# Second gate's logits from scaled, split 16-bit rows, in 16-bit transposes and products, tiles staggered in beats

## The chip, the cores and the metric

One core of one Trainium2 chip. The metric is the device time of one execution in microseconds, median of several runs. The core has five engines, each with an instruction queue that runs in order: TensorE (PE; PEld is its weight load), VectorE (DVE), ScalarE (ACT), GpSimd (POOL) and SyncE (SP, which here issues transfers).

## What is computed

Local attention, then a dense mixture of experts with gates from a Sinkhorn iteration, then a second mixture that routes each row to one expert under a capacity. N = 2304 rows of D = 512, E = 8 experts, hidden size F = 1024.

```python
def _moe2_ref(x, w_gate, w1, w2):
    logits = x @ w_gate
    order = np.argsort(-logits.flatten())
    ...
    for idx in order:
        tok, e = (int(idx) // E, int(idx) % E)
        if assigned[tok] >= 0 or counts[e] >= cap:
            continue
        assigned[tok] = e
        counts[e] += 1
    ...
    for e in range(E):
        mask = assigned == e
        h = np.maximum(x[mask] @ w1[e], 0.0)
        out[mask] = h @ w2[e]
```

x of this function is the output of the dense mixture, `out += P[:, e:e+1] * (relu(x @ w1[e]) @ w2[e])` over the eight experts. The change touches `logits = x @ w_gate` and the form in which x is written out for the routed rows.

## The kernel before, in words

The 2304 rows stand as 18 tiles of 128 rows (NT = 18), three tiles to a block (TB = 3). The dense mixture runs expert by expert. `layer1s` (L845) is a first layer in 192-column products of 16-bit high and low halves (`prod`, L865), whose partial sums ScalarE evacuates as `sa`, `sb`, `sc` and writes out as the 16-bit `hh`, while VectorE writes the low half `hl` (L746, L747). `layer2` (L943) makes 24 products of 128x512 for one tile, and VectorE adds the scaled result to the 32-bit accumulator `acc` (L959). After the last expert, number 7, a tile of `acc` is final and is noted in `finals`.

The gate of the second mixture is made beside expert 7, from three places:

- `held_gate` (L1012) goes over the last six tiles (HELD, tiles 12 to 17) before expert 7 has been added to them, and puts partial logits into `lgh`. `held_weights` and `held_logits` later add expert 7's share, so that the logits of these tiles are there before the tiles are.
- `finish_all` (L973) goes over tiles 0 to 11 as they become final: `gate2` for the logits, then `to_rows`.
- `rest` (L1557) does `to_rows` for the six held tiles, at the end of expert 7, beside the start of the routing.

`gate2` (L981) does four 32-bit transposes of a tile on TensorE (L986), a ScalarE evacuation into the scratch `tmp[:, 0]` (L987), eight product instructions in 32 bits with the gate's weights (L991) and a VectorE copy of the eight logits (L992). `to_rows` (L994) prepares the row for the routed layer: ScalarE's sum of squares (L998, whose elementwise result goes to the scratch `tmp[:, 1]`), five small VectorE instructions that make a power-of-two scale of it (`norm_pow2`, L312 to L317), a 16-bit scaled copy into a row buffer `st2k` (L1005), a 32-bit scaled copy into `tmp[:, 1]` (L1006), GpSimd's subtraction of the two, which is the low half of the row (L1008), and a transfer to `xrows` in HBM (L1009). There are four buffers `st2k` (L334).

The order of all this is set in program order. The background generators are advanced by ticks: `layer2` ticks after each three products, `stream` 2.3 ticks for each third slot of `layer1s`, and `yield n` in a generator lets n ticks go by. So a yield is a number of the main work's instructions, not a time. From `man.close()` (L1552) on a scheduler orders the instructions: that covers `held_logits`, the routing and `rest`.

## Time and profile before

| | us |
|---|---|
| median of 3 runs | 1948.85 |
| lowest, highest | 1943.12, 1950.79 |
| profiled execution, device time | 1943.79 |
| its span, first to last instruction | 1942.0 |
| TensorE busy | 1859.8 (96%) |
| VectorE busy | 1261.4 (65%) |
| ScalarE busy | 916.1 (47%) |
| GpSimd busy | 110.8 (6%) |
| mean granted TensorE clock | 0.988 |

The span is that of the profiled execution; its device time is 1.79 us longer. Busy shares are means over stages with different limits: the dense mixture's last expert lies around 1420 to 1636 us, the routing and the hand-over to the routed layers at about 1630 to 1660 us, the routed layers behind that. What is worth a microsecond has to be read from the stage in which it lies. A busy time of TensorE from products counts their modelled ends, which overlap; where the text needs what a product costs it takes the distance between starts.

### The profile page before, as it was taken

How to read it: one execution, taken by the hardware profiler on the slowest of the kernel's cores; microseconds unless marked ns; L12 is line 12 of the kernel's file. 1: busy time of each engine (PE TensorE's matmuls, PEld its weight loads, DVE VectorE, ACT ScalarE, POOL GpSimd, SP SyncE). 2: the span in 40 equal slices, each digit the busy share in tenths (PEclk: the TensorE clock that was granted, in tenths of full speed). 3: DMA queues.
4: the chain of work that ended last, by engine and by line, in shares of the span. 5: the costliest groups of instructions: out<-in, count | busy, mean ns of one | idle time of the engine just before them, and what ended most of it. 6: DMA issues, size and time to landing. Idle time of an engine off the chain costs nothing.

```text
span 1942.0 us, 39658 instructions
## 1 busy us (share of the span) xinstructions
PE 1859.8 (96%) x15605; PEld 1339.3 (69%) x15605; DVE 1261.4 (65%) x3845; ACT 916.1 (47%) x2493; POOL 110.8 (6%) x142
## 2 busy tenths in 40 slices
PE   6899999999999999999999999999999997899987
PEld 5777755776686766767766867677686773676765
DVE  7877796464666676676667666766747777465540
ACT  6777634552455555554554555455534442222222
POOL 0000000000000000000000000000000113223231
PEclk9999999999999999999999999999999998899999
DMA  8465301140134323323442434234231101435451
GB/s 188 89 131 120 83 1 44 59 160 1 55 120 143 119 93 118 138 88 116 145 136 83 131 117 145 93 99 157 88 104 28 43 20 64 175 123 172 159 211 29
DMA packets 172795, 203.32 MB, mean 105 GB/s; under 512 B 83000, under 2 KB 130104, under 8 KB 168512
## 3 DMA queue, kind: packets, MB, share of 16 engines
q1 hardware_dynamic: 164928, 157.78, 27.4%
q0 software_dynamic: 7680, 43.02, 6.3%
q8 instruction: 122, 2.00, 0.4%
q14 instruction: 65, 0.53, 0.1%
HBM read 143.05 MB, written 57.71 MB: 103 GB/s over the span
## 4 chain that ended last, share of the span: by engine, by line
PE 71%; DVE 11%; issue 6%; DMA 5%; ACT 4%; POOL 2%; SPq 0%; POOLq 0%; ACTq 0%; DVEq 0%
PE p L943 28%; PE p L865 17%; PE pb L865 12%; PE p L1302 4%; PE p L773 3%; DMA w2scr<-st2k 2%; DVE st2k L347 1%; DMA raw<-xrows,idx 1%; PE pb L1152 1%; DVE xl L645 1%; PE p L1314 1%; DMA raw<-in_moe_w_dram 1%; DMA ws<-st2k 1%; PE pb L632 1%; DVE pn L605 1%
## 5 line engine op out<-in xcount | busy, mean ns | idle before, releaser
L943 PE MATMUL p<-w2b,hh 128*128 128x512 f16 x2304 | 686.0, 379 | 0.0
L943 PE MATMUL p<-w2b,hl 128*128 128x512 f16 x1152 | 436.6, 379 | 0.0
L943 PEld LDWEIGHTS <-hh 128*128 128x128 f16 x2304 | 222.1, 99 | 218.2 <-issue 0.2
L865 PEld LDWEIGHTS <-w1b 128*128 128x128 f16 x4032 | 340.3, 98 | 22.2 <-issue 4.0
L865 PEld LDWEIGHTS <-w1x 128*128 128x128 f16 x3024 | 256.3, 98 | 21.1 <-issue 7.4
L865 PE MATMUL p<-th,w1x 128*128 128x192 f16 x1344 | 221.2, 246 | 4.3 <-ACT sa L877 2.2
L865 PE MATMUL pb<-xh,w1b 128*128 128x192 f16 x1344 | 221.3, 246 | 0.0
L943 PEld LDWEIGHTS <-hl 128*128 128x128 f16 x1152 | 112.6, 98 | 135.5 <-issue 0.6
L865 PE MATMUL pb<-xl,w1b 128*128 128x192 f16 x672 | 165.3, 246 | 0.0
L865 PE MATMUL p<-tl,w1x 128*128 128x192 f16 x672 | 165.3, 246 | 0.0
L347 DVE SCALAR_TENSOR_TENSOR st2k<-raw,wsc,st2k 128x512 f16<-128x512 f32 x128 | 91.9, 748 | 51.8 <-ACT st2k L345 51.5
L345 ACT ACTIVATE st2k<-raw,wsc 128x512 f16<-128x512 f32 x128 | 86.5, 713 | 71.3 <-DMA ws<-st2k 58.8
L959 DVE SCALAR_TENSOR_TENSOR acc<-p,SE,acc 128x512 f32<-128x512 f32 x126 | 94.0, 746 | 38.2 <-PE p L943 37.8
L1008 POOL TENSOR_TENSOR st2k<-tmp,st2k 128x512 f16<-128x512 f32 x18 | 24.7, 1370 | 1592.2 <-ACT tmp L1006 1571.1
L746 ACT ACTIVATE hh<-sb 128x192 f16<-128x192 f32 x168 | 61.0, 363 | 111.8 <-DVE sb L909 111.8
L865 PE MATMUL p<-th,w1b 128*128 128x192 f16 x672 | 110.6, 246 | 2.9 <-ACT sc L898 2.9
L746 ACT ACTIVATE hh<-sa 128x192 f16<-128x192 f32 x168 | 60.9, 363 | 107.2 <-DVE sa L883 107.2
L865 PE MATMUL pb<-xh,w1x 128*128 128x192 f16 x672 | 110.6, 246 | 0.0
L865 PE MATMUL p<-xh,w1b 128*128 128x192 f16 x672 | 110.6, 246 | 0.0
L883 DVE TENSOR_TENSOR sa<-pb,sa 128x192 f32<-128x192 f32 x168 | 60.0, 357 | 75.1 <-PE pb L865 72.6
L747 DVE SCALAR_TENSOR_TENSOR hl<-sa,hh 128x192 f16<-128x192 f32 x168 | 60.3, 359 | 72.1 <-ACT hh L746 72.1
L747 DVE SCALAR_TENSOR_TENSOR hl<-sb,hh 128x192 f16<-128x192 f32 x168 | 60.3, 359 | 71.7 <-ACT hh L746 71.7
(309 smaller groups left out, 3381.3 us busy)
## 6 DMA issues: line engine op xcount, KB each, us to landing
raw<-in_moe_w_dram SPq DMA_DIRECT2D x128, 512.0 KB, 5.6
ws<-st2k SPq DMA_DIRECT2D x128, 256.0 KB, 4.5
w2b<-w2scr SPq DMA_DIRECT2D x28, 512.0 KB, 7.1
w2scr<-st2k SPq DMA_DIRECT2D x48, 256.0 KB, 4.5
xrows<-st2k SPq DMA_DIRECT2D x18, 257.0 KB, 3.3
vs<-in_v_dram SPq DMA_DIRECT2D x35, 128.0 KB, 4.1
ldq<-in_q_dram SPq DMA_DIRECT2D x16, 256.0 KB, 4.6
ldk<-in_k_dram SPq DMA_DIRECT2D x16, 256.0 KB, 4.8
```

What stands on the lines that cost most here:

```text
L345: A.activation(hi, src, AF.Copy, scale=sc)
L347: V.scalar_tensor_tensor(lo, src, sc, hi, op0=OP.mult, op1=OP.subtract)
L605: V.tensor_tensor_reduce(pn[:, b, hp], pss[:, hp], mk, 1.0, -3.0e38, OP.add, OP.max, mx[:, u:u + 1])
L746: A.activation(hh[:, f, cols], src, AF.Relu)
L747: V.scalar_tensor_tensor(hl[:, f, cols], src, 0.0, hh[:, f, cols], op0=OP.max, op1=OP.subtract)
L773: PE.matmul(p[:, 0:w], w1v[wi][:, c, fs], x[:, c, ts], start=(n == 0), stop=(n == 3 * DC - 1))
L865: PE.matmul(bank[:, 0:HB], aq[wi][:, c, fs], xq[xi][:, c], start=(start and n == 0), stop=(n == 5), skip_group_check=True)
L883: V.tensor_tensor(t, b3[:, 0:HB], t, OP.add)
L943: PE.matmul(p, h[:, f, js], w2v[wi][:, f], start=(n == 0), stop=(n == 3 * FC - 1))
L959: V.scalar_tensor_tensor(acc[:, i], p, SE[:, e, i:i + 1], acc[:, i], op0=OP.mult, op1=OP.add)
L1008: G.tensor_tensor(xr[:, DM:2 * DM], xs, xr[:, 0:DM], OP.subtract)
L1302: PE.matmul(p[:, 0:CAP], wv1[f // 4][w][:, c, fs], xt[:, x * DC + c], start=(n == 0), stop=(n == 3 * DC - 1))
```

## The change

`gate2` becomes one pass for logits and rows. A tile goes through four steps, each issued one beat (BEAT = 3 ticks) after the one before it: (1) ScalarE's sum of squares; (2) the scale on VectorE, the 32-bit scaled copy, the 16-bit scaled copy, GpSimd's subtraction, and for tiles 0 to 11 the transfer to `xrows`; (3) eight 16-bit transposes of high and low half on TensorE and one ScalarE evacuation of 1024 16-bit values; (4) eight 16-bit products with the gate's weights, which are split in two 16-bit halves once by `gate2_weights` (with a reduction over partitions on GpSimd), and two VectorE instructions that undo the scales. Tiles overlap: with each beat all tiles that are under way take their next step, and a new tile is started. The order inside a beat is that of the tiles, the oldest first.

All 18 tiles pass through steps 1 and 2 here, the six held ones too, with rows that are made for their logits alone; `rest` makes their final rows again in `to_rows`. There the 32-bit copy and GpSimd's subtraction are replaced by one VectorE instruction that reads the accumulator. The 16-bit identity is made earlier.

The diff:

```diff
--- before.py
+++ after.py
@@ -18,6 +18,7 @@
 PR = (4, 0)
 HW = (2, 1)
 LO, W2S, WB = 0, 0, 1
+BEAT = 3
 PXN = 0
 AY, GP, NP_, GL = 2, (1, 0, 1, 1), 18, 1
 WAIT = (1, 1, 1, 1)
@@ -971,49 +972,96 @@
     finals = []
 
     def finish_all():
-        for i in range(HELD[0]):
-            while i not in finals:
-                yield 1
-            yield 4
-            yield from gate2(i, lg2[:, i])
-            yield from to_rows(i)
-
-    def gate2(i, dst):
-
-        xT = rc["tmp"][:, 0]
-        pt = psb.tile([128, 512], F32, name="pb")
-        for c in range(DC):
-            PE.transpose(pt[:, c * 128:(c + 1) * 128], acc[:, i, c * 128:(c + 1) * 128], ident)
+
+        left, on = list(range(HELD[0])), []
+        while left or on:
+            for g in list(on):
+                if next(g, None) is None:
+                    on.remove(g)
+            if left and left[0] in finals:
+                on.append(gate2(left[0], lg2[:, left[0]], True))
+                left.pop(0)
+            yield BEAT
+
+    def gate2_weights():
+
+        m1 = small.tile([128, 1], F32, name="m1g")
+        V.tensor_reduce(m1, wg2s, AX.XY, OP.max, apply_absolute_value=True)
+        mm = small.tile([128, 1], F32, name="mmg")
+        G.partition_all_reduce(mm, m1, 128, bass.bass_isa.ReduceOp.max)
+        yield 4
+        sc = wsc()
+        rc["g2inv"] = rc["pool"].tile([128, 1], F32, name="g2inv")
+        pow2(mm, sc, rc["g2inv"], 1)
+        w = rc["wg2h"] = rc["pool"].tile([128, DC, 2 * E], F16, name="wg2h")
+        V.tensor_scalar(w[:, :, 0:E], wg2s, sc, None, op0=OP.mult)
+        V.scalar_tensor_tensor(w[:, :, E:], wg2s, sc, w[:, :, 0:E], op0=OP.mult, op1=OP.subtract)
+        rc["id16"] = rc["pool"].tile([128, 128], F16, name="id16")
+        V.tensor_copy(rc["id16"], ident)
+        yield 2
+
+    def gate2(i, dst, store):
+
+        m = small.tile([128, 1], F32, name="x2m", bufs=4)
+        xs = rc["tmp"][:, 1]
+        A.activation(xs, acc[:, i], AF.Square, accum_out=m)
+        yield BEAT
+        s = small.tile([128, 1], F32, name="x2s", bufs=4)
+        inv = small.tile([128, 1], F32, name="x2inv", bufs=4)
+        norm_pow2(m, s, inv)
+        xr = st2k()[:, 0:XW]
+        A.activation(xs, acc[:, i], AF.Copy, scale=s)
+        A.activation(xr[:, 0:DM], acc[:, i], AF.Copy, scale=s)
+        G.tensor_tensor(xr[:, DM:2 * DM], xs, xr[:, 0:DM], OP.subtract)
+        if store:
+            V.memset(xr[:, 2 * DM:], 0.0)
+            V.tensor_copy(xr[:, 2 * DM:2 * DM + 2].bitcast(F32), inv)
+            SP.dma_start(xrows[i * 128:(i + 1) * 128, :], xr)
+        yield BEAT
+        xT = rc["tmp"][:, 0].bitcast(F16)
+        pt = psb.tile([128, 512], F32, name="pb").bitcast(F16)
+        for c in range(2 * DC):
+            PE.transpose(pt[:, c * 128:(c + 1) * 128], xr[:, c * 128:(c + 1) * 128], rc["id16"])
         A.activation(xT, pt, AF.Copy)
-        yield 3
+        yield BEAT
         pl = psb.tile([128, 512], F32, name="pb")
-        for c in range(DC):
-            PE.matmul(pl[:, 0:E], xT[:, c * 128:(c + 1) * 128], wg2s[:, c], start=(c == 0), stop=(c == DC - 1))
-        V.tensor_copy(dst, pl[:, 0:E])
+        for c in range(2 * DC):
+            n = 2 * E if c < DC else E
+            PE.matmul(pl[:, 0:n], xT[:, c * 128:(c + 1) * 128], rc["wg2h"][:, c % DC, 0:n], start=(c == 0), stop=(c == 2 * DC - 1))
+        t = small.tile([128, 2 * E], F32, name="lgt")
+        V.tensor_scalar(t, pl[:, 0:2 * E], inv, rc["g2inv"], op0=OP.mult, op1=OP.mult)
+        V.tensor_add(dst, t[:, 0:E], t[:, E:2 * E])
 
     def to_rows(i, x=1):
 
         xs = rc["tmp"][:, x]
-        m = small.tile([128, 1], F32, name="x2m")
+        m = small.tile([128, 1], F32, name="x2m", bufs=4)
         A.activation(xs, acc[:, i], AF.Square, accum_out=m)
-        s = small.tile([128, 1], F32, name="x2s")
-        inv = small.tile([128, 1], F32, name="x2inv")
+        s = small.tile([128, 1], F32, name="x2s", bufs=4)
+        inv = small.tile([128, 1], F32, name="x2inv", bufs=4)
         norm_pow2(m, s, inv)
         xr = st2k()[:, 0:XW]
         V.memset(xr[:, 2 * DM:], 0.0)
         V.tensor_copy(xr[:, 2 * DM:2 * DM + 2].bitcast(F32), inv)
         A.activation(xr[:, 0:DM], acc[:, i], AF.Copy, scale=s)
-        A.activation(xs, acc[:, i], AF.Copy, scale=s)
         yield 1
-        G.tensor_tensor(xr[:, DM:2 * DM], xs, xr[:, 0:DM], OP.subtract)
+        V.scalar_tensor_tensor(xr[:, DM:2 * DM], acc[:, i], s, xr[:, 0:DM], op0=OP.mult, op1=OP.subtract)
         SP.dma_start(xrows[i * 128:(i + 1) * 128, :], xr)
 
 
 
     def held_gate():
-        for i in HELD:
-            yield from gate2(i, lgh[:, i - HELD[0]])
-            yield 2
+        yield from gate2_weights()
+        on = []
+        left = list(HELD)
+        while left or on:
+            for g in list(on):
+                if next(g, None) is None:
+                    on.remove(g)
+            if left:
+                i = left.pop(0)
+                on.append(gate2(i, lgh[:, i - HELD[0]], False))
+            yield BEAT
         bg.done.add("lgh")
 
     def held_weights():
@@ -1090,8 +1138,6 @@
         V.tensor_scalar(rc["tri"], rc["jp"], 0.0, None, op0=OP.is_gt)
         rc["ones"] = lp.tile([128, 128], F16, name="ones16")
         V.memset(rc["ones"], 1.0)
-        rc["id16"] = lp.tile([128, 128], F16, name="id16")
-        V.tensor_copy(rc["id16"], ident)
         for nm, shape, val in (("spacer", [1, 1], 0.0), ("cap", [128, E], float(CAP)), ("ob", [128, E], 0.0), ("un", [128, NT], 1.0),
                                ("AA", [128, 2, NT, E], 0.0), ("zero", [128, NT], 0.0)):
             rc[nm] = lp.tile(shape, F32, name=nm)
```

Below are three places of the order. In the changed kernel's rows L1007 is the sum of squares, L313 to L318 the scale, L1013 the 32-bit and L1014 the 16-bit scaled copy, L1015 GpSimd's subtraction, L1024 the transposes, L1025 their evacuation, L1030 the products and L1048 the subtraction on VectorE; the lines of the first and the second layer are one higher than before (L866, L944), and so are L878, L890, L899 and L747, the evacuations of the first layer.

ScalarE, before, in the stage of the held tiles, from one tile's evacuation to the next:

```order
L987 ACTIVATE tmp<-pb 128x512
L746 ACTIVATE hh_79<-p_17488 128x192
L746 ACTIVATE hh_79<-sc 128x192
L889 ACTIVATE sb<-p_17566 128x192
L746 ACTIVATE hh_79<-sb 128x192
L898 ACTIVATE sc<-p_17566 128x192
L877 ACTIVATE sa<-p_17634 128x192
L746 ACTIVATE hh_79<-sa 128x192
L746 ACTIVATE hh_79<-p_17566 128x192
L746 ACTIVATE hh_79<-sc 128x192
L889 ACTIVATE sb<-p_17634 128x192
L987 ACTIVATE tmp<-pb 128x512
```

ScalarE, after the change, in the same stage, one beat and the start of the next:

```order
L1025 ACTIVATE tmp<-pb 128x1024
L1013 ACTIVATE tmp<-acc,x2s 128x512
L1014 ACTIVATE st2k<-acc,x2s 128x512
L1007 ACTIVATE tmp,x2m<-acc 128x512
L747 ACTIVATE hh_79<-sb 128x192
L899 ACTIVATE sc<-p_17623 128x192
L878 ACTIVATE sa<-p_17725 128x192
L747 ACTIVATE hh_79<-sa 128x192
L747 ACTIVATE hh_79<-p_17623 128x192
L747 ACTIVATE hh_79<-sc 128x192
L1025 ACTIVATE tmp<-pb 128x1024
L1013 ACTIVATE tmp<-acc,x2s 128x512
L1014 ACTIVATE st2k<-acc,x2s 128x512
```

Where one instruction for a tile stood among the first layer's evacuations, there are now four for three different tiles: an evacuation, two copies of the next tile, and the sum of squares of the tile after that. The sum of squares stands right behind the copy for which GpSimd's subtraction waits, and writes the half of `tmp` that the subtraction reads.

VectorE, after the change, in the stage of the finished tiles, at the first of them (`SE` and `junk` belong to other work; L960 is the accumulator's update, L884 and L748 serve the first layer):

```order
L960 SCALAR_TENSOR_TENSOR acc<-p_18235,SE,acc 128x512
L1076 SCALAR_TENSOR_TENSOR junk,w2g<-raw,st2k 128x512 x5
L960 SCALAR_TENSOR_TENSOR acc<-p_18272,SE,acc 128x512
L313 TENSOR_SCALAR pbn<-x2m 128x1
L314 TENSOR_SCALAR pbn<-pbn 128x1
L316 TENSOR_SCALAR pcn<-pbn 128x1
L317 TENSOR_SCALAR x2s<-pcn 128x1
L318 TENSOR_SCALAR x2inv<-pcn 128x1
L1017 MEMSET st2k 128x2
L1018 COPY st2k<-x2inv 128x1
L1076 SCALAR_TENSOR_TENSOR junk,w2g<-raw,st2k 128x512 x3
L884 TENSOR_TENSOR sa<-pb,sa 128x192
```

The scale of tile 0 stands behind the accumulator's update of the next tile, which waits for TensorE's product `p_18272`. On TensorE nine products of the second layer stand between that product's last instruction and the eight transposes of tile 0; between the scale of tile 2 and its transposes there are six.

GpSimd, before, at the change to the routing (L1193 and L1258 are its transfers):

```order
L1089 IOTA jpr 128x128
L1327 MEMSET spacer 1x1 x24
L1008 TENSOR_TENSOR st2k<-tmp,st2k 128x512 x3
L1193 DMA xh<-ws_120,widx 128x4096
L1008 TENSOR_TENSOR st2k<-tmp,st2k 128x512 x3
L1258 DMA raw<-xrows,idx 96x1028 x3
```

GpSimd, after the change, at the same place:

```order
L1137 IOTA jpr 128x128
L1373 MEMSET spacer 1x1 x24
L1239 DMA xh<-ws_120,widx 128x4096
L1304 DMA raw<-xrows,idx 96x1028 x3
L1239 DMA xh<-ws_121,widx 128x4096
```

The six subtractions of the held tiles' rows are gone from GpSimd's queue, where three of them stood ahead of a transfer of weights and three behind it. On VectorE each is one L1048 among the routing's instructions.

## Rows read from the trace of the kernel before

**Rows 1.** The page, part 4: the chain that ended last, by engine.

```profile
PE 71%; DVE 11%; issue 6%; DMA 5%; ACT 4%; POOL 2%; SPq 0%; POOLq 0%; ACTq 0%; DVEq 0%
```

**Rows 2.** Table by stage: busy us per engine (with counts), clock, DMA share, GB/s.

```profile
core 0: us, PE busy (x) PEld busy (x) DVE busy (x) ACT busy (x) POOL busy (x), PEclk, DMA share, GB/s
1420.00:1450.00 30.00, 29.75 (x314) 27.75 (x313) 12.60 (x40) 13.88 (x42) 0.00 (x0) 1.00 0.34 98
1480.00:1510.00 30.00, 29.55 (x248) 22.05 (x246) 22.45 (x74) 14.09 (x39) 3.97 (x3) 1.00 0.23 42
1630.00:1660.00 30.00, 15.23 (x191) 10.10 (x188) 18.73 (x67) 5.73 (x10) 10.72 (x10) 0.68 0.46 160
```

**Rows 3.** Timeline, TensorE, one held tile: start us, us, engine, line, operation, idle before.

```profile
1420.17 0.60 PE L986 MATMUL pb<-ident,acc 128*128 128x128 f32 x4
...
1420.60 0.59 PE L943 MATMUL p<-w2b,hh 128*128 128x512 f16 x2
...
1421.04 0.38 PE L943 MATMUL p<-w2b,hl 128*128 128x512 f16 x1
...
1421.25 0.25 PE L865 MATMUL p<-xh,w1b 128*128 128x192 f16 x1
...
1421.42 0.33 PE L865 MATMUL p<-xh,w1b 128*128 128x192 f16 x2
...
1423.54 0.95 PE L991 MATMUL pb<-wg2s,tmp 128*128 128x8 f32 x8
...
1424.35 0.24 PE L865 MATMUL p<-th,w1x 128*128 128x192 f16 x1
```

**Rows 4.** Timeline, TensorE: 16-bit products at 1598 us, 16-bit transposes at 1722 us.

```profile
1598.29 0.34 PE L1052 MATMUL pb<-w2h,hh 128*128 128x16 f16 x8
...
1598.49 0.34 PE L1054 MATMUL pb<-w2h,hl 128*128 128x8 f16 x8
...
1722.79 0.51 PE L1277 MATMUL pb<-id,raw 96*128 96x96 f16 x8 [0.49 <-DMA raw<-xrows,idx]
...
1723.14 0.29 PE L1314 MATMUL p<-hh,w2b 128*128 128x288 f16 x1
```

**Rows 5.** Groups of ScalarE by shape, whole run: count, busy us, mean ns, idle before.

```profile
L1281 ACT ACTIVATE xgt<-pb 128x768 f16<-128x768 f16 x16 | 13.0, 811 | 42.0 <-PE pb L1277 13.6 <-issue 11.7 <-PE p L1314 10.5
...
L998 ACT ACTIVATE tmp<-acc 128x512 f32<-128x512 f32 x18 | 11.2, 624 | 20.3 <-DVE acc L959 17.7 <-DVE tot L1214 2.6
```

**Rows 6.** Timeline, ScalarE: four evacuations of the first layer, first and last start.

```profile
1435.28 0.36 ACT L746 ACTIVATE hh<-sa 128x192 f16<-128x192 f32 x1 [1.46 <-DVE sa L883]
...
1436.24 0.60 ACT L987 ACTIVATE tmp<-pb 128x512 f32<-128x512 f32 x1
```

**Rows 7.** Timeline, a tile of the finish stage on VectorE, ScalarE and GpSimd.

```profile
1471.02 0.14 DVE L312 TENSOR_SCALAR pbn<-x2m 128x1 int32<-128x1 int32 x1
...
1471.77 0.72 ACT L1005 ACTIVATE st2k<-acc,x2s 128x512 f16<-128x512 f32 x1 [2.35 <-DVE x2s L316]
...
1472.39 0.71 ACT L1006 ACTIVATE tmp<-acc,x2s 128x512 f32<-128x512 f32 x1
...
1472.52 0.75 DVE L959 SCALAR_TENSOR_TENSOR acc<-p,SE,acc 128x512 f32<-128x512 f32 x1
...
1473.18 1.69 POOL L1008 TENSOR_TENSOR st2k<-tmp,st2k 128x512 f16<-128x512 f32 x1 [1469.12 <-ACT tmp L1006]
...
1473.90 1.52 DVE L1028 SCALAR_TENSOR_TENSOR junk<-raw,st2k 128x512 f16<-128x512 f32 x1
```

**Rows 8.** One line's instructions, GpSimd's subtraction: minimum/median/maximum ns.

```profile
L1008 POOL TENSOR_TENSOR st2k<-tmp,st2k x18: 1146/1164/1911, 1473.2 to 1642.7; 128x512 f16<-128x512 f32 x18
```

**Rows 9.** Timeline, GpSimd: the reduction over partitions and the next subtraction.

```profile
1593.58 0.38 POOL L1035 PARTITION_ALL_REDUCE mm<-m  x1 [9.88 <-DVE m L1033]
...
1601.06 1.15 POOL L1008 TENSOR_TENSOR st2k<-tmp,st2k 128x512 f16<-128x512 f32 x1 [7.09 <-issue]
```

**Rows 10.** Timeline, GpSimd, tail: the last subtraction, and the gather.

```profile
1642.66 1.50 POOL L1008 TENSOR_TENSOR st2k<-tmp,st2k 128x512 f16<-128x512 f32 x1 [5.03 <-issue]
...
1647.88 1.37 POOL L1258 DMA_INDIRECT raw<-xrows,idx  x1 [3.72 <-DVE k L1164]
```

**Rows 11.** Table by stage, 5 us of the tail, columns as in rows 2.

```profile
1645.00:1650.00 5.00, 1.99 (x40) 1.60 (x40) 2.63 (x9) 0.00 (x0) 1.82 (x2) 0.50 0.17 56
```

## The prediction

> **What bounds the kernel now.** I read four views. The chain of waits comes first: TensorE carries 71% of it [rows 1], so a microsecond that TensorE spends or idles counts as one, as long as no other engine takes over. The table by stage comes second, for the stretch from 1420 to 1600 us in which all the gate work of the second MoE stands: TensorE is busy 29.75 of 30 us at granted clock 1.00, ScalarE 13.88, VectorE 12.60, GpSimd 0.00 [rows 2]. In the tail, 1630 to 1660, TensorE is half idle. So in the gate stretch TensorE never waits, and the reader is to ask of the change two things: how many microseconds it takes off TensorE, and whether it puts in TensorE's queue an instruction that waits. The third view is the timeline of one tile's gate on TensorE [rows 3], the fourth the groups and the timeline of the helpers' instructions, ScalarE, VectorE and GpSimd, that the transposes will now stand behind [rows 5 to 8].
>
> **What TensorE saves.** One tile's four 32-bit transposes hold TensorE from 1420.17 to 1420.60, 0.43 us, and its eight 32-bit products from 1423.54 to 1424.35, 0.81 [rows 3]: 1.24 us. Now there are eight 16-bit transposes and eight 16-bit products. Eight products of 16 or 8 columns take 0.20 us (1598.29 to 1598.49); eight transposes of 96 columns take 0.35 (1722.79 to 1723.14) [rows 4], so with 128 columns between 0.35 and 0.35 x 128/96 = 0.47; I take 0.43. New sum 0.63, saving 0.61 a tile, **-11.0 us** for 18 tiles (bounds 0.57 and 0.69 a tile: -10 to -12.5).
>
> **What now stands before the transposes.** Before, they read the accumulator, final for long; nothing but TensorE's own turn was needed. Now their data comes through a chain: sum of squares (ScalarE), power-of-two scale (VectorE), 32-bit and 16-bit scaled copies (ScalarE), subtraction (GpSimd), and only then the transposes: the first four need the 16-bit copy, the last four the subtraction. From the rows: scale 0.75 (1471.02 to the start of the copy at 1471.77), first copy 0.62 (start to start), second 0.71, then 0.08 to GpSimd's start [rows 7], whose subtraction takes 1.15 to 1.91 us, median 1.16 [rows 8], the long ones beside VectorE work (1.69 at 1473.18, where the VectorE instruction beside it took 1.52 [rows 7]). Sum 0.75 + 0.62 + 0.71 + 0.08 + 1.16 = 3.3 us at the least, 4.1 with the longest. The change puts one beat (three ticks) between issuing this step and issuing the transposes. In the second layer a tick is three matmuls of 0.22 (two in 1420.60 to 1421.04 [rows 3]), so a beat is 1.9 us; in the first layer, products of 0.08 (two in 1421.25 to 1421.42 [rows 3]), 18 or 36 of them stand between, 1.5 or 3.0 us. The lead is shorter than the chain, and TensorE's queue is in order: it waits, and all its products with it.
>
> **Twelve tiles of the finish stage.** The order shows three kinds, four of each, one per tile of a block. (a) The tile whose scale is issued right behind the accumulator update of the tile after it: that update (0.75, row 1472.52 shows the same form; it frees VectorE after 0.66) waits for TensorE's last product, so the chain starts 0.2 + 0.66 later and ends 4.2 us after that product, while TensorE comes to the transposes after nine matmuls, 1.9 to 2.2 us: stall 2.0 to 2.5. (c) The tile with six matmuls (1.3 us) between scale and transposes: 3.3 - 1.3 = 2.0, say 1.9 to 2.4. (b) The tile between, in a first-layer stretch: its transposes come in time, but ScalarE's evacuation of the next product stands behind the two scaled copies (1.33 us), and a product waits for the bank: 0.5 to 1.15. Sum 4 x (2.25 + 2.15 + 0.8) = 20.8; I take **+20** (15 to 25).
>
> **Six held tiles, a beat at a time.** Here ScalarE becomes the bound. One beat holds, in its order: evacuation of the transposes, 1024 values of 16 bits, estimated from 0.81 for 768 [rows 5] at 1.05, 0.95 start to start; two copies 0.62 + 0.71; then the next tile's sum of squares, which writes the same half of the scratch that the subtraction just issued reads, so ScalarE waits for GpSimd, 0.08 + 1.16 to 1.9; the sum itself, 0.62 [rows 5], its short read-out left uncounted; and on average four evacuations of the first layer, 0.24 each (four in 1435.28 to 1436.24 [rows 6]), 0.96. That is 5.1 to 5.9 us. TensorE has 27 products (mean of 18 and 36), 2.25, and the gate's 0.63: 2.9. Each of five beats stalls 2.2 to 3.0, and the first tile's chain 3.3 - 1.5 = 1.8. Sum 12.8 to 16.8; **+15**. Without the wait for GpSimd ScalarE would still need 3.9 against 2.9.
>
> **The rest.** The weights' split adds eight small VectorE instructions and a reduction over partitions on GpSimd. Such a reduction left GpSimd without work for 7.09 us ahead of its next subtraction [rows 9]; the first new subtraction comes over 10 us later and VectorE is 42% busy [rows 2], so nothing waits: 0 to +0.5. The last tile of the finish stage meets the second such pause as it did before; its transposes now wait for it too: 0 to +2, I take 0.5. In the tail the six subtractions leave GpSimd for VectorE. The last one (1642.66, 1.50 us [rows 10]) becomes one of 0.75 with no second ScalarE copy (0.7) ahead of it, so the last rows can leave 1.4 us earlier; against that, six instructions of 0.75 enter VectorE's queue among the routing's steps, which the gather at 1647.88 [rows 10] also waits for. Ends -2 and +3; I take **-1**. The low halves' order on SP is unchanged; six extra row buffers turn over in the held stage, each free again once transposed: 0.
>
> **Sum.** -11 + 20 + 15 + 0.5 - 1 = +23.5 us. Against the profiled execution, 1943.79 (span 1942.0 and 1.79 around it), 1967.3. That execution lies 5.06 below the median of the runs; from the median it would be 1972.4. I predict 1970, between them: slower by 1.1%.
>
> **Rivals.**
> - *Same: the helpers run ahead.* An engine whose queue holds nothing that waits for TensorE can be early. If ScalarE and VectorE do the chains of kinds (b) and (c) a beat ahead, eight stalls go and 8 to 10 of the 20 us stay; with the held stage at 13 the sum is -12 + 9 + 13 = +10, or less where both run ahead: 1950 to 1957. For it: VectorE has 7.5 free us in 30 [rows 2]. Against it: both queues hold an evacuation of TensorE's product every microsecond. Chance 0.14.
> - *Faster: the lead suffices.* One mechanism: the chain's 3.3 us fits because the transposes reach TensorE's head later than I count from the order. Then TensorE saves 11, the tail 1: 1937. It decides below a chain of 2.2 us in the finish stage and a ScalarE beat below 3.5 us in the held one. The rows show 3.3 and 5.1. Chance 0.14.
> - *Slower still: the clock falls.* In the tail TensorE, 40% busy, was granted 0.50 of its clock, which is its 1.2 GHz level [rows 11]; with stalls every beat, the held stage is 55% busy and the finish stage 83%. At half clock the held beat's TensorE work, 5.8, passes ScalarE's 5.1 by little; a tenth of the finish stage's 134 us at that level adds 13: 1983 to 1986. Chance 0.12, within slower. The Trainium skill, TensorE: Matmul & The Clock Gate, section "HAM oscillation", describes this: where waits recur between short stretches of products, each stretch starts at the low clock again. By that rule the time would be the upper one.
> - *The change does nothing it says:* the order shows the new instructions in place, so I give it no chance.
>
> **How the numbers follow.** A measurement of this kernel tells about 0.5% from no change, 9.7 us. Stalls of 35 us less the saving give slower unless they come out under 21; that holds 0.72 (0.12 of it with the lower clock), same 0.14, faster 0.14. The slower case alone spans, by its bounds, -12.5 - 2 + 15 + 13 = +13.5 to -10 + 25 + 17 + 2.5 + 3 = +37.5, from the middle of the two bases, 1946.3, 1960 to 1984. The range takes in the same case and most of the slower clock: 1944 to 1985; left out are the faster rival and a little above.
>
> **What would show it.** Right: in the profile after, TensorE's waits name GpSimd's subtraction and the 16-bit copy ahead of the transposes, about 2 us in eight tiles; ScalarE's sum of squares waits for GpSimd in the held stage; TensorE's busy share from 1420 on falls to 55% for some 35 us. Wrong: TensorE busy over 97% there, transposes that wait for nothing, or a gate that costs TensorE more than 0.7 us a tile.

## The result, and the profile after

| | before | after |
|---|---|---|
| median, us | 1947.44 (4 runs) | 1970.51 (4 runs, 1969.25 to 1972.41) |
| ratio to before | | 1.0121, interval 1.0098 to 1.0143 |
| profiled execution: device time, span | 1943.79, 1942.0 | 1970.27, 1968.5 |
| mean granted clock | 0.988 | 0.984 |

The change makes the kernel slower by 1.2%: 23 us by the medians, 26.5 by the two profiled executions. The first part of the page of the kernel after:

```profile
PE 1862.7 (95%) x15677; PEld 1334.0 (68%) x15677; DVE 1271.7 (65%) x3906; ACT 930.5 (47%) x2511; POOL 109.5 (6%) x143
```

TensorE's busy time went up by 2.9 us although its work went down; a first sign that it worked at a lower clock for some of the time. The table by stage of the kernel after, columns as in [rows 2]:

```profile
1420.00:1450.00 30.00, 23.69 (x226) 20.23 (x225) 12.09 (x55) 17.13 (x43) 3.46 (x3) 0.89 0.26 81
1450.00:1480.00 30.00, 24.16 (x245) 20.58 (x245) 16.31 (x59) 16.18 (x44) 3.46 (x3) 0.89 0.07 19
1480.00:1510.00 30.00, 27.16 (x241) 19.62 (x240) 21.97 (x72) 13.09 (x35) 2.79 (x2) 1.00 0.13 28
```

From 1420 to 1450 us TensorE was busy 29.75 us at clock 1.00 [rows 2] and is now busy 23.69 at 0.89; from 1480 to 1510 it was 29.55 and is 27.16. Up to 1418 us nothing differs: the accumulator's update that starts there stands 0.2 us later. TensorE's waits from 1400 to 1640 us (total us, times, longest us):

```profile
PE pb L1024 <- POOL st2k L1015: 10.4, 11, 1.3
PE pb L1024 <- ACT st2k L1014: 6.8, 8, 1.0
PE p L866 <- ACT sc L899: 6.0, 3, 3.7
PE p L866 <- ACT sb L890: 5.8, 7, 1.6
```

These four make 29.0 us; one more, of 0.5 us, stands ahead of the accumulator's last update at 1667.78. In the kernel before the same list, up to its last update at 1637.90, makes 5.6 us. Of these, 2.0 lie before 1600, and 3.6 belong to the routing, behind it; the two longest entries are:

```profile
PE pb L1217 <- DVE tot L1214: 1.4, 1, 1.4
PE pb L986 <- DVE acc L959: 1.4, 3, 0.5
```

In the kernel after, the two upper lines are the transposes' chain, the two lower ones are products of the first layer, kept from a bank that ScalarE had not evacuated. A beat of the held stage in the timeline (start us, us, engine, line, operation, idle before):

```profile
1446.37 0.63 ACT L1007 ACTIVATE tmp<-acc 128x512 f32<-128x512 f32 x1 [1.26 <-POOL st2k L1015]
...
1449.71 0.71 ACT L1014 ACTIVATE st2k<-acc,x2s 128x512 f16<-128x512 f32 x1
1450.49 1.15 POOL L1015 TENSOR_TENSOR st2k<-tmp,st2k 128x512 f16<-128x512 f32 x1 [4.15 <-ACT st2k L1014]
1451.68 0.63 ACT L1007 ACTIVATE tmp<-acc 128x512 f32<-128x512 f32 x1 [1.26 <-POOL st2k L1015]
...
1452.31 0.31 ACT L899 ACTIVATE sc<-p 128x192 f32<-128x192 f32 x1
...
1452.67 0.32 PE L866 MATMUL p<-th,w1b 128*128 128x192 f16 x1 [3.66 <-ACT sc L899]
```

From one sum of squares to the next it takes 5.31 us. The second stands behind GpSimd's 1.15 us (idle 1.26), the evacuation L899 behind that, and TensorE's product waits 3.66 us for it. This beat is one of the short ones: the five between the first sum of squares (1427.99) and the sixth (1460.67) take 6.22, 5.22, 6.94, 5.31 and 8.99 us, 6.5 in the mean. In these 32.7 us ScalarE waits 6.4 us for GpSimd, 4.3 for VectorE (the scale and its part of the first layer) and 1.1 for TensorE. A tile of the finish stage, kind (a) of the prediction:

```profile
1522.79 0.38 PE L944 MATMUL p<-w2b,hl 128*128 128x512 f16 x1
...
1523.20 0.75 DVE L960 SCALAR_TENSOR_TENSOR acc<-p,SE,acc 128x512 f32<-128x512 f32 x1
...
1523.87 0.14 DVE L313 TENSOR_SCALAR pbn<-x2m 128x1 int32<-128x1 int32 x1
...
1524.67 0.72 ACT L1013 ACTIVATE tmp<-acc,x2s 128x512 f32<-128x512 f32 x1 [3.92 <-DVE st2k L1017]
...
1525.30 0.71 ACT L1014 ACTIVATE st2k<-acc,x2s 128x512 f16<-128x512 f32 x1
...
1526.06 0.40 PE L1024 MATMUL pb<-id,st2k 128*128 128x128 f16 x4 [0.95 <-ACT st2k L1014]
1526.08 1.15 POOL L1015 TENSOR_TENSOR st2k<-tmp,st2k 128x512 f16<-128x512 f32 x1 [7.46 <-ACT st2k L1014]
...
1527.29 0.40 PE L1024 MATMUL pb<-id,st2k 128*128 128x128 f16 x4 [0.83 <-POOL st2k L1015]
```

The tile's last product ends at 1523.17 and the update starts at 1523.20; scale, two copies and the subtraction follow. TensorE reaches the transposes before them, and waits 0.95 us for the copy and then 0.83 for the subtraction. What the gate costs TensorE where it does not wait, at full clock:

```profile
1508.64 0.61 PE L1024 MATMUL pb<-id,st2k 128*128 128x128 f16 x8
...
1509.09 0.59 PE L944 MATMUL p<-w2b,hh 128*128 128x512 f16 x2
...
1493.47 0.34 PE L1030 MATMUL pb<-wg2h,tmp 128*128 128x16 f16 x8
...
1493.67 0.24 PE L866 MATMUL p<-th,w1x 128*128 128x192 f16 x1
```

Eight transposes 0.45 us (1508.64 to 1509.09), eight products 0.20, together 0.65 against 1.24 before [rows 3].

Last, the clock, in stretches of 2 us, columns as in [rows 2]:

```profile
1430.00:1432.00 2.00, 2.00 (x26) 1.84 (x23) 1.47 (x8) 1.18 (x4) 0.00 (x0) 1.00 0.00 0
1432.00:1434.00 2.00, 0.46 (x5) 0.23 (x4) 0.00 (x0) 0.94 (x2) 0.97 (x1) 1.00 0.00 0
...
1436.00:1438.00 2.00, 2.00 (x15) 1.89 (x14) 0.96 (x7) 1.95 (x3) 0.00 (x0) 0.50 0.00 0
1450.00:1452.00 2.00, 0.00 (x0) 0.00 (x0) 0.00 (x0) 0.74 (x2) 1.15 (x1) 0.93 0.00 0
...
1454.00:1456.00 2.00, 2.00 (x22) 1.92 (x21) 0.93 (x4) 0.73 (x3) 0.00 (x0) 0.50 0.00 0
1562.00:1564.00 2.00, 0.50 (x5) 0.23 (x4) 1.93 (x5) 1.00 (x2) 0.92 (x1) 1.00 0.00 0
...
1566.00:1568.00 2.00, 2.00 (x14) 1.82 (x13) 0.00 (x0) 0.85 (x3) 0.00 (x0) 0.55 0.00 0
```

TensorE was busy 2.00 of 2 us at clock 1.00 at 1430, 0.46 of 2 at 1432 and 0.00 at 1450, 0.50 of 2 at 1562; behind each of these it is busy throughout at 0.50 to 0.55, at or near its 1.2 GHz level. There two products of the second layer take 0.85 us from start to start (1564.65 to 1565.50), where they took 0.44 before [rows 3]. So at granted clock c a busy time b is counted as work of c x b, and (1 - c) x b as lost. Over stretches of 2.5 us that makes 5.9 us from 1420 to 1480 and 4.9 us from 1480 to 1640; in the kernel before it is 0.0 from 1420 to 1620.

How the time adds up, as the shift of three landmarks against the trace of before:

| landmark | before | after | shift |
|---|---|---|---|
| accumulator's update at the start of the held stage | 1418.43 | 1418.61 | +0.2 |
| its update behind the held stage [rows 7] | 1472.52 | 1486.16 | +13.6 |
| its last update | 1637.90 | 1667.78 | +29.9 |
| the span's end | 1942.0 | 1968.5 | +26.5 |

By terms, up to the last update: TensorE saves 18 x 0.59 = 10.6, waits add 29.5 - 5.6 = 23.9, the clock 10.8, together +24.1 of the 29.7. Part of the other 5.6 is in how the list counts a wait: it starts at the modelled end of the product ahead, which lies 0.16 us behind the start of a next one (a product of 0.25 us, 0.08 from start to start [rows 3]); for 21 more waits that is 3.4 us, an estimate. The rest is open. The tail gives back 3.4.

This sums up TensorE's time and does not say what each term costs. In the held stage the low clock cost nothing that the runs show. The run with ready data (below) has the same sums of squares on ScalarE, beat by beat, while its clock falls less. The second and the fifth beat, changed kernel first, columns as in [rows 2]:

```profile
1434.21:1439.43 5.22, 4.53 (x34) 4.19 (x35) 1.74 (x9) 3.91 (x9) 1.15 (x1) 0.67 0.00 2
1451.68:1460.67 8.99, 7.10 (x64) 6.58 (x63) 3.28 (x14) 5.15 (x13) 1.15 (x1) 0.62 0.09 31
```

```profile
1433.46:1438.68 5.22, 1.65 (x18) 1.50 (x18) 1.74 (x9) 3.91 (x10) 1.15 (x1) 1.00 0.01 2
1450.91:1459.91 9.00, 6.33 (x74) 6.03 (x74) 3.28 (x14) 5.05 (x12) 1.15 (x1) 0.81 0.08 31
```

The beats last the same, at clock 0.67 or 1.00, and all five take 32.7 us in both runs: ScalarE sets the time, and TensorE works slowly where it would else wait. In the finish stage the low clock does cost its time. Three runs wait there almost alike, the changed kernel, held tiles as before, and own scratch: TensorE is idle 17.8, 17.5 and 18.0 us between the landmarks, and loses 4.7, 6.4 and 8.0 to the clock; the stage takes 181.6, 183.1 and 185.1.

### The profile page after: what moved, and what is told of

Same layout as the page of the kernel before. It is cut to its first block, busy times and chain, and to the rows that moved or that the text cites. A ratio compares the mean times of both kernels' runs of the same rounds, so it can differ in the third digit from the quotient of the medians.

```text
span 1968.5 us, 39893 instructions
## 1 busy us (share of the span) xinstructions
PE 1862.7 (95%) x15677; PEld 1334.0 (68%) x15677; DVE 1271.7 (65%) x3906; ACT 930.5 (47%) x2511; POOL 109.5 (6%) x143
## 5 line engine op out<-in xcount | busy, mean ns | idle before, releaser
L944 PE MATMUL p<-w2b,hh 128*128 128x512 f16 x2304 | 688.8, 380 | 0.0
L944 PE MATMUL p<-w2b,hl 128*128 128x512 f16 x1152 | 437.7, 380 | 0.0
L944 PEld LDWEIGHTS <-hh 128*128 128x128 f16 x2304 | 221.8, 99 | 219.3 <-issue 1.3
L866 PEld LDWEIGHTS <-w1b 128*128 128x128 f16 x4032 | 343.3, 99 | 30.2 <-issue 10.6
L866 PEld LDWEIGHTS <-w1x 128*128 128x128 f16 x3024 | 258.5, 98 | 28.2 <-issue 14.4
L866 PE MATMUL p<-th,w1x 128*128 128x192 f16 x1344 | 223.3, 247 | 11.2 <-ACT sb L890 8.1
L866 PE MATMUL pb<-xh,w1b 128*128 128x192 f16 x1344 | 223.7, 248 | 0.0
L944 PEld LDWEIGHTS <-hl 128*128 128x128 f16 x1152 | 112.9, 98 | 135.6 <-issue 1.8
L866 PE MATMUL pb<-xl,w1b 128*128 128x192 f16 x672 | 166.6, 248 | 0.0
L866 PE MATMUL p<-tl,w1x 128*128 128x192 f16 x672 | 166.3, 247 | 0.0
L960 DVE SCALAR_TENSOR_TENSOR acc<-p,SE,acc 128x512 f32<-128x512 f32 x126 | 94.1, 746 | 39.3 <-PE p L944 38.6
L866 PE MATMUL p<-th,w1b 128*128 128x192 f16 x672 | 111.0, 247 | 8.6 <-ACT sc L899 8.5
L747 ACT ACTIVATE hh<-sb 128x192 f16<-128x192 f32 x168 | 60.9, 363 | 112.1 <-DVE sb L910 112.1
L884 DVE TENSOR_TENSOR sa<-pb,sa 128x192 f32<-128x192 f32 x168 | 59.9, 356 | 82.4 <-PE pb L866 76.1
L866 PE MATMUL p<-xh,w1b 128*128 128x192 f16 x672 | 112.1, 248 | 0.0
L866 PE MATMUL pb<-xh,w1x 128*128 128x192 f16 x672 | 112.0, 248 | 0.0
L748 DVE SCALAR_TENSOR_TENSOR hl<-sa,hh 128x192 f16<-128x192 f32 x168 | 61.1, 364 | 76.0 <-ACT hh L747 76.0
L748 DVE SCALAR_TENSOR_TENSOR hl<-sb,hh 128x192 f16<-128x192 f32 x168 | 60.2, 358 | 77.1 <-ACT hh L747 77.1
L747 ACT ACTIVATE hh<-sa 128x192 f16<-128x192 f32 x168 | 60.9, 363 | 103.0 <-DVE sa L884 103.0
L774 PE MATMUL p<-xh,w1b 128*128 128x384 f16 (+1 forms) x512 | 101.5, 288 | 4.5 <-DVE hl L756 4.3
```

The costliest lines, as they stand in the source:

```text
L747: A.activation(hh[:, f, cols], src, AF.Relu)
L748: V.scalar_tensor_tensor(hl[:, f, cols], src, 0.0, hh[:, f, cols], op0=OP.max, op1=OP.subtract)
L774: PE.matmul(p[:, 0:w], w1v[wi][:, c, fs], x[:, c, ts], start=(n == 0), stop=(n == 3 * DC - 1))
L866: PE.matmul(bank[:, 0:HB], aq[wi][:, c, fs], xq[xi][:, c], start=(start and n == 0), stop=(n == 5), skip_group_check=True)
L884: V.tensor_tensor(t, b3[:, 0:HB], t, OP.add)
L944: PE.matmul(p, h[:, f, js], w2v[wi][:, f], start=(n == 0), stop=(n == 3 * FC - 1))
```

## The experiments

Medians are compared with runs of the kernel before on the same chip: 1947.37 us for the first four runs, 1936.22 for the next four, 1946.38 for the last three. "Held", "finish" and "end" are the shifts against the trace of before between the landmarks of the table above (start to second, second to last update, last update to the span's end; the end only where the chip's runs of before are as in that trace). The kernel before, profiled again on another chip, has 54.08 and 165.52 us between these landmarks, where the first trace has 54.09 and 165.38. One offset has to be known: in the kernel before the second landmark, an update on VectorE, also has the first finished tile's gate (1.24 us) and five products of the second layer (1.1) ahead of it, which come behind it in the later kernels. So held tiles that cost as much as before show as -2.6 under "held", with as much too much under "finish" (in the beat of 6 two more products lie ahead of it). The changed kernel's held stage is longer by 16.1 us, its finish stage by 13.6.

| run | median, us | ratio to before, interval | held | finish | end |
|---|---|---|---|---|---|
| changed kernel | 1970.51 | 1.0121 (1.0098 to 1.0143) | +13.5 | +16.2 | -3.4 |
| beat of 6 | 1963.73 | 1.0090 (1.0073 to 1.0107) | +15.0 | -2.6 | +7.2 |
| low half on VectorE | 1948.28 | 1.0009 (0.9999 to 1.0020) | +3.7 | +5.3 | -2.7 |
| own scratch | 1966.11 | 1.0094 (1.0073 to 1.0114) | +6.5 | +19.7 | -4.0 |
| ready data | 1957.48 | 1.0059 (1.0036 to 1.0083) | +13.5 | +3.0 | -3.4 |
| tail's part alone | 1935.62 | 0.9998 (0.9984 to 1.0012) | 0.0 | -0.9 | |
| held tiles as before | 1947.38 | 1.0058 (1.0035 to 1.0081) | -2.6 | +17.7 | |
| held as before, VectorE, beat of 4 | 1930.97 | 0.9977 (0.9967 to 0.9987) | -2.6 | -1.2 | |
| all tiles, VectorE, beat of 4 | 1936.09 | 1.0001 (0.9989 to 1.0013) | +1.2 | -1.4 | |
| held as before, VectorE, beat of 4, last tiles at 3 | 1939.56 | 0.9969 (0.9955 to 0.9983) | -2.6 | +2.1 | -6.1 |

My theory: TensorE's in-order queue reaches the transposes before the chain of scale, two copies and subtraction on three engines is through (finish stage), and ScalarE, which waits for GpSimd in each beat, is the bound of the held stage. Rivals: ScalarE's load alone, whatever the lead; or a 16-bit gate that saves TensorE nothing.

**A longer lead.**

```diff
-BEAT = 3
+BEAT = 6
```

> BEAT 6 instead of 3, all else as changed. Theory A (lead too short: the chain of scale, two copies and subtraction, 3.3 us, is longer than the 1.3 to 2.2 us that TensorE needs to reach the transposes): a beat is now 3.9 us in the second layer, so the waits at the transposes of the finish stage (13.5 of its 17 us of waits) fall under 3 us, the held stage's waits under 6, and the low clock that follows them goes for the most part: 1942 to 1950. Theory B (ScalarE simply has too much work for these tiles, whatever the lead): the same work in the same stage, 1962 to 1970. Theory C (the 16-bit gate costs TensorE no less than the 32-bit one): not below 1950.

Measured 1963.73: missed by 14 us, and the parts tell why. In the finish stage the longer lead does what the theory says, +16.2 becomes -2.6. The held stage is not helped at all (+15.0); there ScalarE's work for a tile is the same and only stands elsewhere. Of this run's waits from 1400 to 1640 us:

```profile
PE p L866 <- ACT sb L890: 7.9, 2, 4.1
PE pb L1024 <- POOL st2k L1015: 5.8, 8, 1.3
```

One wait for `sb` now lasts 4.1 us. And the end costs 7.2 us in place of giving back 3.4: the transposes of the last three tiles came at 1623.5 to 1631.4 us, behind the products for the held tiles' logits, the routing needs their logits too, and the gather came 15.1 us after the last update (1666.30 against 1651.20) where it was 7.9 in the changed kernel. So theory A holds in one stage, B in the other, and a longer beat has a price at the end that I had not counted.

**The low half on VectorE.**

```diff
-        A.activation(xs, acc[:, i], AF.Copy, scale=s)
         A.activation(xr[:, 0:DM], acc[:, i], AF.Copy, scale=s)
-        G.tensor_tensor(xr[:, DM:2 * DM], xs, xr[:, 0:DM], OP.subtract)
+        V.scalar_tensor_tensor(xr[:, DM:2 * DM], acc[:, i], s, xr[:, 0:DM], op0=OP.mult, op1=OP.subtract)
```

> The low half by one VectorE instruction from the accumulator in all 18 tiles of gate2; the 32-bit copy and GpSimd's subtraction are gone, BEAT 3. Theory A: the chain is 0.75 + 0.71 + 0.1 + 0.75 = 2.3 us against leads of 1.3 to 2.2, the finish stage's waits fall from 17 to 4 to 7 us; ScalarE's beat in the held stage falls from 5.1 to 3.3 us against TensorE's 2.9, its waits from 12 to 2 to 4; the clock stays at its upper level: 1940 to 1947. Theory B: the held stage gains as much, the finish stage only what the copy's 0.6 us give: 1953 to 1960.

1948.28, 1 us above what A allowed and 5 below what B did. The run takes 9.8 us off the held stage and 10.9 off the finish stage. It shortens the chain, and it also takes ScalarE's copy and its wait for GpSimd away, so for the held stage it does not tell the one from the other: the five beats there take 22.7 us in place of 32.7. TensorE's waits from 1400 to 1600 us and the table by stage:

```profile
PE pb L1023 <- ACT st2k L1013: 5.1, 7, 1.0
PE p L866 <- ACT sb L890: 4.0, 10, 1.5
PE p L866 <- ACT sc L899: 3.8, 3, 1.8
PE pb L1023 <- DVE st2k L1016: 2.7, 7, 0.4
```

```profile
1420.00:1450.00 30.00, 24.47 (x286) 21.20 (x284) 17.92 (x72) 18.36 (x49) 0.08 (x1) 1.00 0.27 84
1450.00:1480.00 30.00, 26.16 (x234) 18.36 (x232) 21.72 (x73) 12.43 (x35) 0.00 (x0) 1.00 0.06 15
```

Up to 1640 us it still waits 18.6 us, but the clock stays at 1.00 throughout, also where TensorE is busy only 24.47 of 30 us: the 10.8 us of the low clock are gone together with part of the waits.

**A scratch of its own for the sum of squares.**

```diff
-        A.activation(xs, acc[:, i], AF.Square, accum_out=m)
+        xr = st2k()[:, 0:XW]
+        A.activation(xr[:, DM:2 * DM], acc[:, i], AF.Square, accum_out=m)
```

> The sum of squares writes its elementwise result into the row buffer's low half (16 bits) instead of the half of the scratch that GpSimd reads, so that ScalarE does not wait for GpSimd there. Theory A (both the lead and ScalarE's wait): ScalarE's beat in the held stage loses 1.2 us, held waits from 12 to 6 to 8 us, less low clock there, finish stage as it was: 1962 to 1966. If ScalarE's wait for GpSimd was the whole of the held stage's loss: 1955. If it cost nothing: 1970.

1966.11: at the upper end of A. The held stage gives back 7.0 us, and the five beats take 25.0 us in place of 32.7: ScalarE's wait for GpSimd was a little under half of the held stage's 16.1. In the finish stage no sum of squares had waited for GpSimd; its waits stay, and it takes 3.5 us more (+19.7) because the clock falls for longer there, 8.0 us lost and not 4.7.

**Transposes that wait for nothing.**

```diff
-            PE.transpose(pt[:, c * 128:(c + 1) * 128], xr[:, c * 128:(c + 1) * 128], rc["id16"])
+            PE.transpose(pt[:, c * 128:(c + 1) * 128], rc["id16"], rc["id16"])
```

> The transposes read the 16-bit identity, ready since long, instead of the row; every other instruction stays, so what is left out is that TensorE waits for the row's chain (and the logits are not those of the rows). Theory A: the waits at the transposes go, 13.5 us in the finish stage and 4 in the held one; what ScalarE delays (its evacuations sb and sc behind the copies, 10 us) stays; some low clock stays: 1945 to 1953. Theory B: 1962 or more. Theory C: the gate without waits shows on TensorE what it costs, at least 1.2 us a tile.

1957.48: better than the changed kernel by 13 us, yet 4.5 above the range. The finish stage falls from +16.2 to +3.0, as A has it. The held stage stays at +13.5, where A had 4 us of it go: TensorE no longer waits at the transposes, and waits instead at the first layer's products, as this run's list shows:

```profile
PE p L866 <- ACT sb L890: 12.8, 8, 2.4
PE p L866 <- ACT sc L899: 9.8, 4, 3.7
```

There the wait at a transpose was never the cause, only the place where TensorE met ScalarE's backlog. Theory C was wrong from the start: a gate that does not wait takes 0.65 us, as the rows above show.

**The tail's part alone**, in the kernel before:

```diff
-            G.tensor_tensor(xr[:, DM:2 * DM], xs, xr[:, 0:DM], OP.subtract)
+            V.scalar_tensor_tensor(xr[:, DM:2 * DM], acc[:, i], s, xr[:, 0:DM], op0=OP.mult, op1=OP.subtract)
```

(for tiles 12 to 17, without their 32-bit copy)

> The kernel before with one part of the change alone: the low half of the six held tiles' rows by one VectorE instruction, without the 32-bit copy and GpSimd's subtraction. The prediction's term was -1 us (ends -2 and +3): 1946 to 1947. In the changed kernel the tail gave back 3.4 us; if this part is the cause, 1944; if that came from routing work that was done while TensorE waited for the gates, no difference from before, or slower.

0.9998: no difference in 10 runs. Its profile had the gather earlier, so I took the kernel before and this one again, on one chip.

> The kernel before, unchanged, for its profile beside the next run's on the same chip: the gather 10 us after the accumulator's last update.

> The kernel with the tail's part alone, again, for its profile beside that of the kernel before: the gather 8 us after the last update and 3 us earlier than there. If the gather sets the end, the span is 2 to 3 us shorter; if what follows waits for something else, the spans agree within 1 us.

The first gather, in the kernel before and with the tail's part alone:

```profile
1650.52 1.26 POOL L1258 DMA_INDIRECT raw<-xrows,idx  x1 [3.82 <-DVE k L1164]
```

```profile
1644.09 1.29 POOL L1262 DMA_INDIRECT raw<-xrows,idx  x1 [12.97 <-DVE fl L1159]
```

The accumulator's last update was at 1640.4 and 1636.2, so the gap fell from 10.1 to 7.9 us as expected. The two executions differ by 3.5 us before the held stage is reached; with that taken off, the first expert's gather is 2.9 us earlier, the second's 0.8, those of the third to the sixth 4.1 to 4.2, and that of the seventh, at 1861.23 and 1857.72, not at all. In between the second kernel's transposes of gathered rows waited for longer than any such wait of the first there (0.8):

```profile
1825.82 0.82 PE L1281 MATMUL pb<-id,raw 96*128 96x96 f16 x8 [2.13 <-DMA raw<-xrows,idx]
```

The spans, 1945.1 and 1941.7, differ by 3.4 us, which is the difference at the start. One execution each: that the gain is always given back there is not shown. The medians, with an interval of -3.1 to +2.3 us, show no gain, and leave room for one of up to 3.1.

**The held tiles by the 32-bit gate of before**, the rest as changed:

```diff
         yield from gate2_weights()
-        on = []
-...
+        for i in HELD:
+            yield from gate2_old(i, lgh[:, i - HELD[0]])
+            yield 2
```

> The changed kernel with the six held tiles' partial logits by the 32-bit transposes and products of before; the weights' split and the finish stage stay as changed (GpSimd, BEAT 3). Theory A (two separate losses): the held stage's 15.8 us go, the finish stage's 14 to 16 and the tail's -3 stay: 1957 to 1961. If the held stage caused the waits of the finish stage too (a backlog carried on): 1947 to 1950.

1.0058, 11.2 us above the kernel before on its chip, where 1957 to 1961 meant 10 to 14. The held stage's loss is gone (the -2.6 is the offset of the landmark), and the finish stage's +17.7 stands as in the changed kernel, with 1.7 us more lost to the low clock: two separate losses, no backlog carried from the one to the other. The table by stage, held and finish:

```profile
1420.00:1450.00 30.00, 30.00 (x308) 26.88 (x305) 14.34 (x49) 13.78 (x42) 0.38 (x1) 1.00 0.36 112
1480.00:1510.00 30.00, 26.98 (x244) 19.43 (x242) 22.04 (x77) 13.67 (x36) 3.29 (x2) 1.00 0.22 36
```

**Putting it together.** Held tiles as before, low half on VectorE, `BEAT = 4`:

> Held tiles by the 32-bit gate of before; finish stage with the low half on VectorE straight from the accumulator and BEAT 4, so that the lead (2.6 us in the second layer) covers the chain (2.3). Theory A: the 12 tiles save 12 x 0.61 = 7.3 us on TensorE, waits of 2 to 4 us are left, the tail gives 0 to -3: 1938 to 1944, faster than both. Theory C (TensorE saves nothing): 1947 to 1951.

0.9977 (0.9967 to 0.9987): 4.5 us below the kernel before by the ratio, and below the changed kernel by more than 1%. It is the first version that beats both. The stages:

```profile
1420.00:1450.00 30.00, 30.00 (x326) 28.40 (x325) 15.04 (x51) 14.94 (x45) 0.00 (x0) 1.00 0.32 99
1480.00:1510.00 30.00, 28.46 (x250) 19.37 (x249) 23.10 (x83) 12.49 (x32) 0.00 (x0) 1.00 0.25 45
```

Its finish stage waits 6.5 us in all, where 2 to 4 were expected. All 18 tiles in 16 bits, with the 16-bit copy of the held ones on VectorE too:

> All 18 tiles by the 16-bit gate, low half on VectorE, BEAT 4 everywhere, and in the held stage the 16-bit copy on VectorE too, so that ScalarE keeps the sum of squares, the evacuation and the first layer's own: about 2.7 to 3 us a beat against TensorE's 3.5 to 3.9. Theory A: 18 x 0.61 = 11 us saved, 4 to 7 us of waits left, tail 0 to -3: 1938 to 1944. If VectorE becomes the bound of the held stage in ScalarE's place: 1946 to 1952.

1.0001, no gain. The held stage:

```profile
1420.00:1450.00 30.00, 25.89 (x312) 23.61 (x311) 21.00 (x78) 16.64 (x52) 0.00 (x0) 1.00 0.27 81
```

VectorE rose from 12.60 to 21.00 of 30 us, and TensorE is busy 25.89: the held stage costs 3.8 us more than with the 32-bit gate (+1.2 against -2.6), although the six tiles save TensorE 3.5. TensorE is idle 6.6 us there in place of 0.4, nearly twice the saving, and most of its waits name evacuations of ScalarE. Whether VectorE holds these up, and so is the bound, is not shown. Last, the better one with the last block's tiles at a beat of 3:

```diff
-        yield BEAT
+        yield BEAT if i < 9 else 3
```

> As the run with 32-bit held tiles, low half on VectorE and BEAT 4, but with BEAT 3 for the last block's tiles 9 to 11, whose logits the routing waits for. There the gather came 11.5 us after the accumulator's last update, against 8.0 where BEAT was 3. If tile 11's later steps set the start of the routing: the gap is 8 to 9 us again, 1 to 2 us of waits come back at the last three tiles, 7 to 8 us below the kernel before (ratio 0.9955 to 0.9965). If something else sets the gather: 5 us below it, as without this.

0.9969 (0.9955 to 0.9983), 6.0 us below the kernel before. The gap from last update to gather fell from 11.5 to 7.6 us, as theory had it, but the three tiles' waits took 3 of them back where 1 to 2 were expected, so the 7 to 8 us were missed; against 0.9977 the gain is inside the intervals.

## Why the prediction was right, point by point

The forecast, 1970, slower by 1.1%, stands at 1970.51. Its direction and its mechanism are shown by the runs. That the sum comes out so close is partly luck: two terms were too small and two too large.

- *TensorE's saving*, 0.61 a tile: 0.59 measured. Right.
- *Finish stage*, +20 and 0.5 for the last tile: its waits make 17.1 us. Kind (a), 2.0 to 2.5: 1.78 to 1.85. Kind (c), 1.9 to 2.4: 2.01 to 2.03, on three tiles. Kind (b), 0.5 to 1.15: 0.56 to 0.99. The fourth tile of kind (c), the last one, behind the second reduction, was counted at 2.15 and 0.5 and waited 0.44. Kind (a) was sized too long: 4.2 less 1.9 to 2.2 is 2.0 to 2.3, and the first four transposes run for 0.2 us between its two waits. In kind (c) the subtraction took 1.63 to 1.65 us beside VectorE's work and not the 1.16 of the sum, which made up for the same 0.2. Undoing the lead (beat of 6) or the wait itself (ready data) took most of the loss away.
- *Held stage*, +15: its waits make 11.9 us, and waits and low clock together, which here share one time, 17.8. That ScalarE and its wait for GpSimd set the beat is shown by the own scratch (-7.0) and by the ready data (no gain). The beat was mis-sized: 5.1 to 5.9 us forecast, 6.5 in the mean, since it counted ScalarE's wait for GpSimd but none for VectorE, which was 4.3 us in five beats. The forecast's sign, TensorE busy 55% for some 35 us, failed as written: from 1430 to 1465 it was busy 24.05 of 35 us, 69%, at clock 0.80, which is the work of 55%.
- *Clock*, 0 in the sum and 13 in a rival with a chance of 0.12: it fell, and TensorE lost 10.8 us to it. The 5.9 in the held stage hid behind ScalarE's beat; the 4.9 in the finish stage came on top, where the rival had 13. So about 5 us belonged in the sum. The row of before that pointed at it, TensorE 40% busy at 0.50 [rows 11], did not size it: the clock fell behind the waits of a stage in which TensorE is busy 90%.
- *Tail*, -1: -3.4 by the two traces, while the part alone changes nothing in the median (0.9998, down to -3.1 us by its interval). Of the 3.4 the gather accounts for 2.1 (7.9 us after the last update and not 10.0); the rest is open.
- *The rest*, +0.5: the reduction at 1419.5 us and GpSimd's pause behind it kept nobody waiting; the first subtraction came at 1433.0.

So -10.6, +17.1, +17.8, +4.9 and -3.4, together +25.8, took the place of -11, +20.5, +15, 0 and -1. (The 5.6 us of waits that stood in the kernel before and the 5.6 that the terms above leave over cancel in it.) The prediction's "TensorE never waits" in the gate stretch of before is off by the 2.0 us of the list above, and its 13.88, 12.60 and 0.00 us of the helpers, named for 1420 to 1600, are those of 1420 to 1450; from 1480 to 1510 VectorE is busy 22.45 [rows 2].

The rival "helpers run ahead" fell: but for the last tile, the waits came within half a microsecond of those read off the order, tile by tile. The Trainium skill, TensorE: Matmul & The Clock Gate, section "HAM oscillation", describes a kernel whose waits are longer than the stretches of products between them, and in which each next stretch starts at the low clock. The waits here are shorter than the stretches, and the rows agree in part: the clock fell to 0.50 from 1436 to 1438 behind the waits at 1432, and in the run with the low half on VectorE the waits recur and it stays at 1.00. With the rival's clock the time was put at 1983 to 1986; the clock fell, but in the finish stage it cost 4.9 us and not 13.

## What to carry to other kernels

A cheaper instruction on the bounding engine is worth its saving only if its operands are ready when the queue reaches it: count, in instructions of that queue, the lead that the program order gives, and compare it with the chain of producers on the other engines. Where a stage's helper is near its limit, the wait shows up at whatever instruction meets its backlog; moving the wait away from one place (ready data) shows whether that place was the cause. Size such a helper's beat with its own waits for every other engine in it. And ask, stage by stage, what a low clock on TensorE costs: its time in a stage that TensorE bounds, and nothing that these runs show in one that a helper bounds.

## What the runs showed of the hardware

- Waits can bring the low clock or not: with 29.0 us of them in the changed kernel TensorE lost 10.8 us to it, with 18.6 us in the run with the low half on VectorE 0.0.
- A low clock costs time only where TensorE bounds the stage: in the finish stage, at 17.5 to 18.0 us of idle time, 4.7, 6.4 and 8.0 us lost make it 181.6, 183.1 and 185.1 us long; the held stage of the changed kernel and of the run with ready data is 67.55 us long with 5.9 and with 4.2 us lost.
- Waits that look alike can go either way: behind 0.95 and 0.83 us at one group of transposes the clock stayed at 1.00 at 1526 us (from 1510 to 1540 nothing is lost), and behind the same pair at 1563 it fell to 0.55. What decides between them is open.
- GpSimd's subtraction and VectorE's instruction L1076 of the changed kernel hold each other up, and the later one pays: a subtraction that started 0.04 to 0.1 us behind such an instruction took 1.59 to 1.65 us in place of 1.15 (1517, 1554, 1592), and the instruction that started behind a subtraction took 1.51 to 1.61 in place of 0.68 (1489, 1526, 1563).
- Chips differ: the kernel before had medians of 1947.4, 1936.2 and 1946.4 us on the chips of these runs, with spreads of 7 to 12 us on each; executions of these kernels differ by up to 3.5 us before 1418 us, where their programs are the same. Medians were compared only within one chip.
